# Attention blocks transposed in pairs, inverse sums spread by transposes, and the end of attention written in another order

## The chip, the core and the metric

The program runs on one of the eight NeuronCores of a Trainium2 chip. The metric is the device time of one execution in microseconds (us). A core has five engines that run side by side and meet at semaphores: TensorE (PE; its weight loads have a row of their own, PEld), VectorE (DVE), ScalarE (ACT), GpSimd (POOL) and SyncE (SP), which here only issues DMAs. Matrix products go to PSUM, which PE alone writes and which DVE and ACT read.

## The reference

```python
q_rot, k_rot = (rotate(q), rotate(k))            # rotary embedding, batch 2, 8 heads, 576 x 64
scores = scale * np.matmul(q_rot, k_rot.transpose(0, 1, 3, 2))
scores = scores - np.max(scores, axis=-1, keepdims=True)
attn = np.exp(scores)
attn = attn / (np.sum(attn, axis=-1, keepdims=True) + 1e-09)
x = np.matmul(attn, v)                           # then (batch * 576) x 512
h = x @ w_in;  x = where(h > 0, h, exp(min(h, 0)) - 1) @ w_out      # 512 -> 2048 -> 512
h = x @ w2_in; out = (h * tanh(softplus(h))) @ w2_out
```

## The kernel before

Heads are worked two at a time: eight pairs `p`, four for each of the two batch entries. A pair has nine score tiles of 128 queries by 576 keys (`TPP = 9`): tile `i` from 0 to 7 is head `i % 2`, query block `i // 2`, and tile 8 holds the last 64 queries of both heads. One loop over steps `u` (nine to a pair) writes the whole attention stage engine by engine in a fixed order; no scheduler moves anything there. In step `u` stand, among others:

- `do_S(u)`: the score product of tile `u` on PE into a PSUM tile `ps_s` (two buffers); `do_max(u)`: the row minimum of the negated scores on DVE (L392); `do_exp(u)`: the exponential on ACT (L400) into `P`, which frees `ps_s`.
- `do_T(u - 3)`: `P` of the tile three steps back is transposed on PE, four blocks of 128 keys into `psT` (L441) and the last 64 keys into a slot of `psL` (L442, output of 64 rows). `do_evac` copies `psT` into `pt` on DVE or ACT (L455, L457), `do_evac_last` copies `psL` for four tiles at a time on DVE (L467).
- `do_av(p, g, c)` (L473): output of group `g` (tiles 0 to 3, or 4 to 8) from key chunk `c` of five. Head 0 goes to PSUM rows 0 to 63 of `psA` and head 1 to rows 64 to 127, 256 columns each in group 0 and 320 in group 1. The table `plan` sets the steps.
- The inverse sums: `do_inverse` on DVE (L409 to L417) forms them and repeats each 64 times into `rw`; `do_spread` (L423) multiplies `rw` with an identity, so that they stand in `psA` along the columns; `do_keep` (L432, ACT) copies that to `R`. The product then uses the same `psA`; `do_x` (L488, DVE) multiplies it by `R` and so frees `psA` for the next spread; `do_xh` and `do_xl` (L492 on ACT, L496 on POOL) split the result in two for the next stage.
- POOL also applies the rotary embedding of later pairs (L273 to L277) and splits them (L298, L299). SP issues, in one queue, the loads of `qk` (L260), of the values `v` (L265), of raw weights, and small copies that wait for POOL's splits (L323, L338, L339).
- Weights of the next stage are prepared a part at a time (`weight_part`), from step 21 on: POOL L95, DVE L99, L103, L107, ACT L121, POOL L122. A job is opened when fewer than two are running, which issues its L95.

The feed-forward layers follow: per step one first product `g1_mm` (24 matmuls, L183) into `ps_s`, the activation, and later second products `g2_first` (L683, 24 matmuls) into `ps_g`. `tail` runs three first products within the last steps of attention.

Of the kernel before, what the change touches and what calls it, by code (L numbers as in the profile page):

```python
# [26 lines left out]
def kernel(  # L27
# [23 lines left out]
    GB, GE, PB = 9, 2, 4  # L51
# [123 lines left out]
    def g1_mm(m, f, b):  # L175
        c = m * NF + f
        hi, lo = WI[c]
        o = ps_s()
# [11 lines left out]

    G = {}
# [19 lines left out]
    def elu(m, f, b, o):  # L211
        h = o[:, :, :HS]
        t, g = tmp("ta"), tmp("tb")
        nc.scalar.activation(out=v2(g), in_=h, func=AF.Relu, scale=-1.0)
        nc.scalar.activation(out=t, in_=g, func=AF.Exp, scale=-1.0)
        nc.scalar.activation(out=g, in_=g, func=AF.Tanh, scale=-0.5)
        nc.vector.scalar_tensor_tensor(out=g, in0=t, scalar=1.0, in1=g, op0=ALU.add, op1=ALU.mult)
        nc.vector.tensor_tensor(out=v2(g), in0=v2(g), in1=h, op=ALU.max)  # L218
        return m, f, b, g
# [10 lines left out]
    def attention(att, ps, tail):  # L230
# [3 lines left out]
        idn2 = att.tile([128, 64], F32, name="idn2")  # L234
        rw = att.tile([128, 3, 2, 64], F32, name="rw")
# [9 lines left out]
        v_t = {}  # L245
        sp_t = {}
# [16 lines left out]
        def load_v(p):  # L263
            v = att.tile([128, 5, 128], F32, tag="v", name="v_t", bufs=2)
            nc.sync.dma_start(out=v, in_=vp[p])  # L265
            v_t[p] = v

# [75 lines left out]
        P_t = {}  # L343
        mn_t = {}
        sm_t = {}
        R_t = {}
        SLOT = (0, 1, 2, 3, 4)
# [47 lines left out]
        def do_exp(u):  # L395
            P = att.tile([128, S], F32, tag="P", name="P", bufs=PB)
            p, i = divmod(u, TPP)
            g, j = (0, i) if i < 4 else (1, i - 4)
# [7 lines left out]
        def do_inverse(p, g):  # L406
# [5 lines left out]
                out=rw[:, 0:2].rearrange("p t h d -> p (t h) d"),  # L412
                in_=r[:, 0:4].unsqueeze(2).to_broadcast([128, 4, 64]).unsqueeze(3), axis=AX.X, op=ALU.add,
            )
            for h in range(2 * g):
                rows = slice(64 * h, 64 * h + 64)
                nc.vector.tensor_reduce(  # L417
                    out=rw[rows, 2, h, :], in_=r[rows, 4:5].to_broadcast([64, 64]).unsqueeze(2), axis=AX.X, op=ALU.add
                )

        def do_spread(p, g):
# [12 lines left out]
        pt_t = [att.tile([128, 2, 5, n], F32, name=f"pt{g}") for g, n in enumerate((256, 320))]  # L434

        def do_T(u):
            P = P_t.pop(u)
            i = u % TPP
            tv = psT[u % 2]
            for c in range(4):  # L440
                nc.tensor.transpose(tv[:, c, :], P[:, c * 128:c * 128 + 128], idn)  # L441
            nc.tensor.transpose(psL[:S - 512, i % 4, :], P[:, 512:S], idn)  # L442
# [16 lines left out]
        def do_evac_last(i):  # L459
            r = S - 512  # L460
            if i < 8:
                o = pt_t[i // 4][:r, :, 4, 0:256].rearrange("p h (t q) -> p h t q", t=2)
                tv = psL[:r].rearrange("p (t h) q -> p h t q", h=2)
            else:
                o = pt_t[1][:r, :, 4, 256:320]
                tv = psL[:r, 0, :].rearrange("p (h q) -> p h q", h=2)
            nc.vector.tensor_copy(out=o, in_=tv)  # L467

        def do_av(p, g, c):
            n = (256, 320)[g]  # L470
            o = psA
            for h in range(2):
                nc.tensor.matmul(  # L473
                    o[64 * h:64 * h + 64, :n],
                    lhsT=v_t[p][:, c, 64 * h:64 * h + 64],
                    rhs=pt_t[g][:, h, c, :],
                    start=(c == 0), stop=(c == 4),
                )
# [7 lines left out]
        def do_x(p, g):  # L486
            x = R_t[p, g]
            nc.vector.tensor_tensor(out=x, in0=psA[:, :(256, 320)[g]], in1=x, op=ALU.mult)  # L488
# [5 lines left out]
        def do_xl(p, g, eng):  # L494
            x, hi, lo = x_parts(p, g)
            eng.tensor_tensor(out=lo, in0=x, in1=plain(hi), op=ALU.subtract)  # L496

# [16 lines left out]
        nc.vector.memset(rw[:, 2], 0.0)  # L514
        nc.vector.tensor_tensor(out=idn2, in0=idn[:, 0:64], in1=idn[:, 64:128], op=ALU.add)
        for t in pt_t:
            nc.vector.memset(t[S - 512:128, :, 4, :], 0.0)
# [56 lines left out]
        for u in range(max(av_at) + 2):  # L574
# [7 lines left out]
            if i == 8 and p + 1 < NP:  # L582
                load_v(p + 1)
            if u == 16:
# [5 lines left out]
            for (pp, g) in ends.get(u - 1, []):  # L590
                do_x(pp, g)
# [10 lines left out]
            for (pp, g, c) in av_at.get(u, []):  # L602
                if g == "r":
                    do_spread(pp, c)
                else:
                    do_av(pp, g, c)
            if u >= NU:
                tail(u - NU, False)
            if 0 <= u - LAG < NU:
# [4 lines left out]
                if j in (3, 7):  # L614
                    do_evac_last(j)
            for (pp, g) in spreads.get(u, []):
# [16 lines left out]
            for (pp, g) in ends.get(u - 1, []) + ends.get(u - 2, []):  # L633
                if (pp, g) in ends.get(u - (2 if g and u < NU else 1), []):
                    do_xh(pp, g)
                    do_xl(pp, g, nc.gpsimd if pp < NP - 1 else nc.vector)
            for _ in range(PARTS.get(u, 0)):
                if njob[0] < 2 * GF:
                    weight_part()
            if u >= NU:  # L640
                tmp_pool[0] = att
                tail(u - NU, True)
# [3 lines left out]
    def moe(mp, early):  # L646
# [19 lines left out]
        g_pool = [None]  # L666
# [70 lines left out]
        def step(n):  # L737
            m, f, b = g1_seq[n]
            o = early.pop(n) if n in early else g1_mm(m, f, b)
            if m == 0:  # L740
                for _ in range(3 if GF <= n < half - 1 else 0):
                    weight_part()
                if o is not None:
                    o = elu(m, f, b, o)
# [124 lines left out]
```

## Time and profile before

| | us |
|---|---|
| runs | 574.50, 574.96, 1397.33 |
| median | 574.96 |
| profiled execution | 570.46 |
| its span, first to last instruction | 568.6 |

In the span PE is busy for 553.9 us (97%), DVE for 376.9, ACT for 277.9, POOL for 238.7. The attention stage takes the first 160 us or so, the feed-forward layers the rest. A matmul's row gives when it started and a modelled end; since matmuls overlap, what one costs is read from one start to the next and not from its duration. An fp32 matmul leaves two records, an fp32 transpose one. "Idle" in brackets behind a row is how long that engine stood still before it, and what let it go on.

### The profile page before, as it was taken

The numbers are of one execution on the slowest core, as the hardware profiler recorded it, in microseconds if no ns is written. First come the engines' busy times: TensorE is split into PE (matmuls) and PEld (weight loads), VectorE is DVE, ScalarE is ACT, GpSimd is POOL, SyncE is SP. The second block draws the span as 40 slices with busy tenths as digits, with TensorE's granted clock in tenths as the row PEclk, the third lists the DMA queues.
The fourth block names the chain that finished last, engine by engine and source line by source line (L and its number), as shares of the span: only waits on it lengthen the run. The fifth ranks groups of instructions, "written<-read, shape, count | busy, mean of one in ns | idle before, by whom it ended". The sixth has DMA issues, their size and how long they took to land.

```text
span 568.6 us, 10131 instructions
## 1 busy us (share of the span) xinstructions
PE 553.9 (97%) x3888; PEld 499.7 (88%) x3888; DVE 376.9 (66%) x607; ACT 277.9 (49%) x512; POOL 238.7 (42%) x227
## 2 busy tenths in 40 slices
PE   7799999999999999999999999999999999999997
PEld 6568677777789999999999999999999998999985
DVE  6666899888846766777777777869844555432222
ACT  3646666667755665455555456435443322322110
POOL 6998999982310323323322331445533332230000
PEclk9999999999999999999999999999999999999999
DMA  6368676655110323223222322234532423000012
GB/s 231 110 197 258 205 228 178 184 143 161 38 39 4 108 80 107 76 76 96 91 74 78 108 75 75 85 115 139 159 116 84 121 88 110 22 14 10 29 65 93
DMA packets 43120, 60.69 MB, mean 107 GB/s; under 512 B 13760, under 2 KB 31936, under 8 KB 42304
## 3 DMA queue, kind: packets, MB, share of 16 engines
q1 hardware_dynamic: 42528, 59.46, 34.2%
q8 instruction: 31, 0.51, 0.4%
q10 hardware_dynamic: 544, 0.59, 0.3%
q14 instruction: 17, 0.14, 0.1%
HBM read 46.20 MB, written 2.36 MB: 85 GB/s over the span
## 4 chain that ended last, share of the span: by engine, by line
PE 85%; DVE 6%; ACT 3%; DMA 2%; issue 1%; POOL 1%; SPq 1%; ACTq 0%; POOLq 0%; DVEq 0%
PE ps_s L183 34%; PE ps_g L683 18%; PE ps_h L712 17%; PE ps_s L385 5%; PE psA L473 5%; PE psT L441 4%; DMA qk_t<-in_qk_dram 2%; PE psA L423 2%; DVE mn L392 1%; ACT P L400 1%; DVE wu L99 1%; PE psL L442 1%; DVE pt L455 1%; DVE R L488 0%; DVE rw L411 0%
## 5 line engine op out<-in xcount | busy, mean ns | idle before, releaser
L392 DVE TENSOR_REDUCE mn<-ps_s 128x1 f32<-128x576 f32 x72 | 53.9, 751 | 19.2 <-PE ps_s L385 15.2
L661 ACT ACTIVATE ta<-ps_s 128x576 f32<-128x576 f32 x32 | 20.8, 649 | 92.7 <-PE ps_s L183 92.6
L400 ACT ACTIVATE P<-ps_s,mn 128x576 f32<-128x576 f32 x72 | 53.1, 739 | 9.5 <-DVE mn L392 6.8
L183 PE MATMUL ps_s<-XH,wi0h 128*128 128x288 f32 x256 | 54.9, 296 | 0.9 <-DVE tb L218 0.9
L99 DVE TENSOR_SCALAR wu<-wu 128x512 int32<-128x512 int32 x64 | 33.7, 527 | 32.9 <-POOL wu L95 32.9
L183 PE MATMUL ps_s<-XL,wi0h 128*128 128x288 f32 x256 | 54.5, 294 | 0.0
L183 PE MATMUL ps_s<-XL,wi1h 128*128 128x288 f32 x256 | 54.4, 294 | 0.0
L183 PE MATMUL ps_s<-XH,wi0l 128*128 128x288 f32 x256 | 54.4, 294 | 0.0
L183 PE MATMUL ps_s<-XH,wi1l 128*128 128x288 f32 x256 | 54.2, 293 | 0.0
L183 PE MATMUL ps_s<-XH,wi1h 128*128 128x288 f32 x256 | 54.1, 293 | 0.0
L122 POOL TENSOR_TENSOR wi1l<-wu,wi1h 128x512 fp32r<-128x512 f32 x16 | 21.4, 1337 | 76.0 <-ACT wi1h L121 76.0
L122 POOL TENSOR_TENSOR wo0l<-wu,wo0h 128x512 fp32r<-128x512 f32 x16 | 21.9, 1366 | 68.3 <-ACT wo0h L121 56.4
L107 DVE SCALAR_TENSOR_TENSOR wu<-raw,wu 128x512 int32<-128x512 int32 x64 | 48.8, 762 | 1.7
L103 DVE SCALAR_TENSOR_TENSOR wu<-raw,wu 128x512 int32<-128x512 int32 x64 | 47.6, 744 | 2.0
L95 POOL TENSOR_SCALAR wu<-raw 128x512 f32<-128x512 f32 x64 | 45.1, 706 | 4.7
L473 PE MATMUL psA<-pt,v_t 128*64 128x256 f32 (+1 forms) x320 | 45.6, 416 | 0.6 <-ACT R L432 0.6
L122 POOL TENSOR_TENSOR wo1l<-wu,wo1h 128x512 fp32r<-128x512 f32 x16 | 22.0, 1375 | 57.2 <-ACT wo1h L121 56.9
L663 DVE TENSOR_TENSOR g<-ta,g 128x576 fp32r<-128x576 f32 x25 | 20.4, 817 | 36.4 <-ACT g L662 36.4
L183 PEld LDWEIGHTS ps_s<-XH,wi0h 128*128 128x128 f32 x256 | 41.4, 188 | 3.2 <-DVE tb L218 1.3
L457 ACT ACTIVATE pt<-psT 128x512 f32<-128x512 f32 x44 | 26.3, 597 | 36.4 <-PE psT L441 36.4
L441 PE MATMUL psT<-idn,P 128*128 128x128 f32 x288 | 43.4, 274 | 0.0
L183 PEld LDWEIGHTS ps_s<-XH,wi1h 128*128 128x128 f32 x256 | 41.8, 188 | 1.2
(146 smaller groups left out, 1409.6 us busy)
## 6 DMA issues: line engine op xcount, KB each, us to landing
raw<-in_w_in_dram SPq DMA_DIRECT2D x32, 512.0 KB, 3.7
raw<-in_w_out_dram SPq DMA_DIRECT2D x32, 512.0 KB, 3.3
qk_t<-in_qk_dram SPq DMA_DIRECT2D x6, 1152.0 KB, 7.2
qa<-qh SPq DMA_DIRECT2D x24, 144.0 KB, 2.6
v_t<-in_vp_dram SPq DMA_DIRECT2D x8, 320.0 KB, 4.3
out_dram<-Y SPq DMA_DIRECT2D x9, 256.0 KB, 2.0
ka<-kh SPq DMA_DIRECT2D x12, 144.0 KB, 2.5
ka<-kl SPq DMA_DIRECT2D x12, 144.0 KB, 2.6
```

The source lines that it names most:

```text
L95: nc.gpsimd.tensor_scalar(out=u, in0=high.bitcast(F32), scalar1=REBASE, scalar2=0.0, op0=ALU.mult, op1=ALU.add)
L99: nc.vector.tensor_scalar(out=ui, in0=ui, scalar1=3, scalar2=0x7FFFFFF8, op0=ALU.logical_shift_left, op1=ALU.bitwise_and)
L103: nc.vector.scalar_tensor_tensor(out=ui, in0=high, scalar=-0x80000000, in1=ui, op0=ALU.bitwise_and, op1=ALU.bitwise_or)
L107: nc.vector.scalar_tensor_tensor(out=ui, in0=low, scalar=29, in1=ui, op0=ALU.logical_shift_right, op1=ALU.bitwise_or)
L122: nc.gpsimd.tensor_tensor(out=lo, in0=u, in1=plain(hi), op=ALU.subtract)
L183: nc.tensor.matmul(o[:, j, :HS], lhsT=w[:, cc, :], rhs=x[:, b, cc, j * HS:j * HS + HS], start=(k == 0), stop=(k == 3 * NC - 1),)
L392: nc.vector.tensor_reduce(out=m, in_=psS[u][:, :, :HS], axis=AX.XY, op=ALU.min)
L400: nc.scalar.activation(out=P.rearrange("p (j n) -> p j n", j=2), in_=psS.pop(u)[:, :, :HS], func=AF.Exp, scale=-1.0, bias=mn_t.pop(u), acc ...
L441: nc.tensor.transpose(tv[:, c, :], P[:, c * 128:c * 128 + 128], idn)
L473: nc.tensor.matmul(o[64 * h:64 * h + 64, :n], lhsT=v_t[p][:, c, 64 * h:64 * h + 64], rhs=pt_t[g][:, h, c, :], start=(c == 0), stop=(c == 4),)
L683: nc.tensor.matmul(o[:, j, :HS], lhsT=w[:, e * 128:e * 128 + 128], rhs=gt[:, i, j * HS:j * HS + HS], start=(k == 0), stop=(k == 3 * GF - 1),)
L712: nc.tensor.matmul(o, lhsT=l, rhs=w, start=(k == 0), stop=(k == 3 * GF - 1))
```

## The change

- `do_T`: two heads' tiles (`i` even, then odd) lie side by side in one `P` buffer of 2 x 576 columns. The odd tile is transposed from column 64 on, so that the last 64 keys of the even tile and the first 64 of the odd one form one block of 128 columns, transposed at once with the odd tile. Tile 8 keeps its own 64-column block. A pair has 41 transposes of `P` in place of 45.
- The keys of head 1 are then in another order, so `load_v` lays its values out likewise, with four DMAs in place of one; tile 8 needs the old order, which `load_vb` loads with one more DMA. In group 1 of `do_av`, head 1's product of 320 columns becomes one of 64 (values `vb`) and one of 256.
- `do_spread` uses transposes for tiles 0 to 3 or 4 to 7, and for tile 8 two 64-column matmuls straight from the inverse; two DVE reductions (L417) go.
- `do_x` of group 1 moves from the following step to the end of its own, ahead of the weight parts. One weight job is opened at step 19.
- At the end of attention the last product goes to `psT[0]`, `tail` splits the activation and places the last `do_x`, `do_xh` and `do_xl` between its parts; the fifth first product uses `ps_g`, second products of the first block start a step later with one step that runs two. One preload of an activation table goes.

```diff
-        o = ps_s()
+        if (m, f, b) == (0, 0, 1):
+            o = g_pool[0].tile([128, 2, 512], F32, tag="g", name="ps_g", bufs=2)
+        else:
+            o = ps_s()
...
-            nc.sync.dma_start(out=v, in_=vp[p])
+            nc.sync.dma_start(out=v[:, :, 0:64], in_=vp[p, :, :, 0:64])
+            nc.sync.dma_start(out=v[0:64, :, 64:128], in_=vp[p, 64:128, :, 64:128])
+            nc.sync.dma_start(out=v[64:128, 0:4, 64:128], in_=vp[p, 0:64, 1:5, 64:128])
+            nc.sync.dma_start(out=v[64:128, 4, 64:128], in_=vp[p, 0:64, 0, 64:128])
...
+        def load_vb(p):
+            vb = att.tile([128, 5, 64], F32, tag="vb", name="vb_t", bufs=1)
+            nc.sync.dma_start(out=vb, in_=vp[p, :, :, 64:128])
...
-            P = att.tile([128, S], F32, tag="P", name="P", bufs=PB)
+                P2_t[p, i // 2] = att.tile([128, 2, S], F32, tag="P", name="P", bufs=PB)
...
         def do_spread(p, g):
-            for t in range(2 + g):
+            r = rc_t.pop((p, g))
+            for t in range(2):
+                nc.tensor.transpose(
+                    psA[:, 128 * t:128 * t + 128], rw[:, 2 * t:2 * t + 2].rearrange("p h d -> p (h d)"), idn
+                )
+            for h in range(2 * g):
                 nc.tensor.matmul(
-                    psA[:, 128 * t:min(128 * t + 128, 256 + 64 * g)],
-                    lhsT=rw[:, t].rearrange("p h d -> p (h d)"), rhs=idn if t < 2 else idn2,
-                    start=True, stop=True,
+                    psA[64 * h:64 * h + 64, 256:320],
+                    lhsT=r[:, 4:5].to_broadcast([128, 64]), rhs=idn[:, 64 * h:64 * h + 64], start=True, stop=True,
                 )
...
             for c in range(4):
-                nc.tensor.transpose(tv[:, c, :], P[:, c * 128:c * 128 + 128], idn)
-            nc.tensor.transpose(psL[:S - 512, i % 4, :], P[:, 512:S], idn)
+                k = k0 + c * 128
+                nc.tensor.transpose(tv[:, c, :], P[:, k:k + 128], idn)
+            if i == TPP - 1:
+                nc.tensor.transpose(psL[:S - 512, 0, :], P[:, 512:S], idn)
+            elif i % 2:
+                P2 = P2_t.pop((p, i // 2)).rearrange("p h k -> p (h k)")
+                nc.tensor.transpose(psL[:, i // 2, :], P2[:, 512:640], idn)
...
+        def av_home(p, g):
+            return psT[0].rearrange("p c q -> p (c q)") if (p, g) == (NP - 1, 1) else psA
...
             for h in range(2):
-                nc.tensor.matmul(
-                    o[64 * h:64 * h + 64, :n],
-                    lhsT=v_t[p][:, c, 64 * h:64 * h + 64],
-                    rhs=pt_t[g][:, h, c, :],
-                    start=(c == 0), stop=(c == 4),
-                )
+                m = n if h == 0 else 256
+                v = v_t[p][:, c, 64 * h:64 * h + 64]
+                if h and g:
+                    w = slice(256, 320)
+                    rhs = pt_t[g][:, h, c, w] if c < 4 else pl_t[g][:, 320:384]
+                    part(h, w, vb_t[p][:, c, :], rhs, True)
+                rhs = pt_t[g][:, h, c, :m] if c < 4 else pl_t[g][:, :m]
+                part(h, slice(0, m), v, rhs, not (h and g))
...
             for (pp, g) in ends.get(u - 1, []):
-                do_x(pp, g)
+                if g == 0:
+                    do_x(pp, g)
...
+            for (pp, g) in ends.get(u, []):
+                if g == 1 and pp < NP - 1:
+                    do_x(pp, g)
...
+            if u == 19:
+                open_job()
...
-                    pend.extend((n + (D1 if n < half - 1 else LATE[e]), (0, (g, b, e))) for e in range(NC))
+                    pend.extend((n + (2 if n < GF else D1 if n < half - 1 else LATE[e]), (0, (g, b, e))) for e in range(NC))
...
-            if n == half - 1:
-                nc.scalar.preload_act_table_set("mish")
```

The order on PE in pair 2's steps, over the product of pair 1's group 1. Before (`ka`, `qa`, `qb`: scores; `pt`: transposed exponentials):

```order
L473 MATMUL psA<-pt_86,v_t 64x320 x4
L385 MATMUL ps_s<-ka,qa 128x288 x2
L385 MATMUL ps_s<-ka,qb_113 128x288 x2
L441 MATMUL psT_82<-idn,P 128x128 x4
L442 MATMUL psL<-idn,P 64x128
L385 MATMUL ps_s<-ka,qa 128x288 x2
L385 MATMUL ps_s<-ka,qb_113 128x288 x2
L441 MATMUL psT_81<-idn,P 128x128 x4
L442 MATMUL psL<-idn,P 64x128
L473 MATMUL psA<-pt_86,v_t 64x320 x6
```

and in the changed kernel:

```order
L509 MATMUL psA<-pt_85,v_t 64x320
L509 MATMUL psA<-pt_85,vb_t 64x64
L509 MATMUL psA<-pt_85,v_t 64x256
L509 MATMUL psA<-pt_85,v_t 64x320
L509 MATMUL psA<-pt_85,vb_t 64x64
L509 MATMUL psA<-pt_85,v_t 64x256
L406 MATMUL ps_s<-ka,qa 128x288 x2
L406 MATMUL ps_s<-ka,qb_117 128x288 x2
L469 MATMUL psT_81<-idn,P 128x128 x4
L474 MATMUL psL<-idn,P 128x128
L406 MATMUL ps_s<-ka,qa 128x288 x2
L406 MATMUL ps_s<-ka,qb_117 128x288 x2
```

Every second tile has lost its transpose into `psL`, the others have one of 128 rows, and each chunk has three matmuls where it had two.

The order on POOL around the first weight preparations (`XL`: the split of the attention output; `qk_t`: rotary embedding of pair 4). Before:

```order
L299 TENSOR_TENSOR ql<-qk_t,qh 128x576
L496 TENSOR_TENSOR XL<-R_557,XH 128x256
L273 TENSOR_TENSOR qk_t<-qk_t,tab 128x576
L275 TENSOR_TENSOR qk_t<-qk_t,tab 128x576
L95 TENSOR_SCALAR wu<-raw 128x512 x2
```

and in the changed kernel:

```order
L318 TENSOR_TENSOR ql<-qk_t,qh 128x576
L540 TENSOR_TENSOR XL<-R_556,XH 128x256
L95 TENSOR_SCALAR wu<-raw 128x512
L292 TENSOR_TENSOR qk_t<-qk_t,tab 128x576
L294 TENSOR_TENSOR qk_t<-qk_t,tab 128x576
```

The first L95 now stands ahead of the embedding of pair 4, not behind two parts of it.

The order on DVE where pair 1's group 1 ends (`rw`: repeated inverse sums, `mn`: row minimum, `R`: output of attention). Before, `do_x` stood behind the weight part L103:

```order
L411 TENSOR_REDUCE rw<-rc 128x256
L392 TENSOR_REDUCE mn<-ps_s 128x1
L455 COPY pt_85<-psT_81 128x4x128
L103 SCALAR_TENSOR_TENSOR wu<-raw,wu 128x512
L488 TENSOR_TENSOR R_691<-psA,R_691 128x320
```

and in the changed kernel ahead of it:

```order
L437 TENSOR_REDUCE rw<-rc 128x256
L413 TENSOR_REDUCE mn<-ps_s 128x1
L487 COPY pt_84<-psT_80 128x4x128
L532 TENSOR_TENSOR R_690<-psA,R_690 128x320
L103 SCALAR_TENSOR_TENSOR wu<-raw,wu 128x512
```

## Rows read from the trace of the kernel before

**Rows 1.** The span in 40 equal slices: PE's busy tenths, and TensorE's granted clock

```profile
PE   7799999999999999999999999999999999999997
PEclk9999999999999999999999999999999999999999
```

**Rows 2.** Busy time in one stretch of attention, then granted clock, DMA share, GB/s

```profile
100.00:120.00 20.00, 19.89 (x152) 15.51 (x149) 17.58 (x32) 13.69 (x33) 17.76 (x16) 1.00 0.58 165
```

**Rows 3.** Who waited for whom: us in total, times, longest

```profile
PEld psA L423 <- DVE R L488: 2.1, 4, 1.0
...
SPq L323 <- POOL kh L298: 36.0, 6, 7.4
```

**Rows 4.** Timeline, steps of pairs 4 and 5: start, duration, engine, line [idle before]

```profile
97.49 0.52 PEld L423 LDWEIGHTS psA<-idn,rw 128*128 128x128 f32 x4 [0.37 <-DVE R L488]
97.49 0.71 PE L423 MATMUL psA<-idn,rw 128*128 128x128 f32 x4
...
97.96 0.51 PE L385 MATMUL ps_s<-ka,qa 128*128 128x288 f32 x2
...
99.21 1.08 PE L473 MATMUL psA<-pt,v_t 128*64 128x256 f32 x8
...
100.23 0.53 PE L385 MATMUL ps_s<-kh,bh 128*128 128x288 f32 x2
...
101.13 0.60 PE L441 MATMUL psT<-idn,P 128*128 128x128 f32 x4
...
101.56 0.27 PE L442 MATMUL psL<-idn,P 128*64 128x128 f32 x1
...
101.59 0.51 PE L385 MATMUL ps_s<-ka,qa 128*128 128x288 f32 x2
...
102.85 1.52 PE L473 MATMUL psA<-pt,v_t 128*64 128x256 f32 x12
...
104.29 0.53 PE L385 MATMUL ps_s<-ka,qa 128*128 128x288 f32 x2
...
106.68 0.78 PE L423 MATMUL psA<-idn,rw 128*128 128x128 f32 x6
...
107.27 0.51 PE L385 MATMUL ps_s<-ka,qa 128*128 128x288 f32 x2
```

**Rows 5.** Timeline, several engines, around the first weight preparation

```profile
45.41 0.43 SPq L260 DMA_DIRECT2D qk_t<-in_qk_dram  x1
...
53.82 1.41 POOL L273 TENSOR_TENSOR qk_t<-qk_t,tab 128x576 f32<-128x576 f32 x1 [0.59 <-DMA qk_t<-in_qk_dram]
...
56.57 1.31 POOL L95 TENSOR_SCALAR wu<-raw 128x512 f32<-128x512 f32 x2
...
57.28 0.87 DVE L99 TENSOR_SCALAR wu<-wu 128x512 int32<-128x512 int32 x1 [2.63 <-POOL wu L95]
...
59.79 0.53 PE L385 MATMUL ps_s<-ka,qa 128*128 128x288 f32 x2 [0.64 <-ACT P L400]
...
61.86 0.71 PE L423 MATMUL psA<-idn,rw 128*128 128x128 f32 x4 [0.73 <-DVE R L488]
```

**Rows 6.** Timeline of POOL: the once-a-pair wait, two pairs running

```profile
83.08 0.88 POOL L496 TENSOR_TENSOR XL<-R,XH 128x320 fp32r<-128x320 f32 x1 [1.09 <-ACT XH L492]
...
100.90 0.87 POOL L496 TENSOR_TENSOR XL<-R,XH 128x320 fp32r<-128x320 f32 x1 [1.09 <-ACT XH L492]
```

**Rows 7.** Timeline of PE: the end of attention, and one wait in mid-program

```profile
165.51 2.91 PE L473 MATMUL psA<-pt,v_t 128*64 128x320 f32 x20 [0.59 <-ACT R L432]
168.35 0.53 PE L183 MATMUL ps_s<-XH,wi0h 128*128 128x288 f32 x2
...
174.57 0.43 PE L183 MATMUL ps_s<-XH,wi0l 128*128 128x288 f32 x2
175.67 0.53 PE L183 MATMUL ps_s<-XH,wi0h 128*128 128x288 f32 x2 [0.67 <-DVE tb L218]
...
354.63 0.53 PE L183 MATMUL ps_s<-XH,wi0h 128*128 128x288 f32 x2 [0.19 <-DVE tb L218]
```

More of the change, by code (lines that the diff above doesn't have):

```diff
@@ L459, in do_evac_last, with part @@
         def do_evac_last(i):
-            r = S - 512
             if i < 8:
-                o = pt_t[i // 4][:r, :, 4, 0:256].rearrange("p h (t q) -> p h t q", t=2)
-                tv = psL[:r].rearrange("p (t h) q -> p h t q", h=2)
-            else:
-                o = pt_t[1][:r, :, 4, 256:320]
-                tv = psL[:r, 0, :].rearrange("p (h q) -> p h q", h=2)
+                g = i // 4
+                o = pl_t[g][:, 0:256].rearrange("p (t q) -> p t q", t=2)
+                tv = psL[:, 2 * g:2 * g + 2, :]
+            else:
+                o = pl_t[1][:S - 512, 256:384]
+                tv = psL[:S - 512, 0, :]
             nc.vector.tensor_copy(out=o, in_=tv)
+        def av_home(p, g):
+            return psT[0].rearrange("p c q -> p (c q)") if (p, g) == (NP - 1, 1) else psA
         def do_av(p, g, c):
             n = (256, 320)[g]
-            o = psA
-            for h in range(2):
-                nc.tensor.matmul(
-                    o[64 * h:64 * h + 64, :n],
-                    lhsT=v_t[p][:, c, 64 * h:64 * h + 64],
-                    rhs=pt_t[g][:, h, c, :],
-                    start=(c == 0), stop=(c == 4),
-                )
+            o = av_home(p, g)
+            def part(h, cols, v, rhs, first):
+                nc.tensor.matmul(
+                    o[64 * h:64 * h + 64, cols], lhsT=v, rhs=rhs,
+                    start=(c == 0 and first), stop=(c == 4), skip_group_check=True,
+                )
+            for h in range(2):
+                m = n if h == 0 else 256
[6 more added lines that the diff above has]
+                part(h, slice(0, m), v, rhs, not (h and g))
         def x_parts(p, g):
@@ L487, in do_x @@
             x = R_t[p, g]
[L488 removed]
+            nc.vector.tensor_tensor(out=x, in0=av_home(p, g)[:, :(256, 320)[g]], in1=x, op=ALU.mult)
         def do_xh(p, g):
@@ L513, in attention @@
             nc.vector.memset(t[:, :, 1:2], 1e-9)
[L514 to L517, printed above, removed]
+        nc.vector.memset(pl_t[1][S - 512:128, 256:384], 0.0)
         for t in qb:
@@ L573, in attention @@
                     ends.setdefault(u, []).append((p, g))
-        for u in range(max(av_at) + 2):
+        for u in range(max(av_at) + 1):
             p, i = divmod(u, TPP)
@@ L583, in attention @@
                 load_v(p + 1)
+            if i == 6 and p < NP:
+                load_vb(p)
             if u == 16:
@@ L641, in attention @@
                 tmp_pool[0] = att
-                tail(u - NU, True)
+                tail(u - NU, 1, last_x)
                 tmp_pool[0] = None
@@ L795, with tail @@
     early = {}
-    def tail(k, late):
-        if late:
-            if k in (2, 3):
-                elu_lo(*elu_hi(*early[k - 2]))
-                early[k - 2] = None
-            if k in (1, 2):
-                early[k - 1] = elu(0, k - 1, 0, early[k - 1])
-        elif k in (0, 1, 3):
-            n = min(k, 2)
-            early[n] = g1_mm(0, n, 0)
+    def tail(k, late, last_x):
+        if not late:
+            if k in (0, 1, 3):
+                n = min(k, 2)
+                early[n] = g1_mm(0, n, 0)
+        elif k == 1:
+            early[0] = elu_join(*elu(0, 0, 0, early[0]))
+        elif k == 2:
+            early[0] = elu_lo(*elu_hi(*early[0]))
+            early[1] = elu(0, 1, 0, early[1])
+        elif k == 3:
+            early[1] = elu_join(*early[1])
+            last_x()
+            early[1] = elu_lo(*elu_hi(*early[1]))
     with tc.tile_pool(name="att", bufs=1, reuse_waits="tile") as att, tc.tile_pool(
```

53 lines of the change are left out of this document (35 added, 18 removed).

## The prediction

> **What bounds the kernel now.** I read the busy slices first. PE is at nine tenths or more in 37 of 40 slices and TensorE's granted clock is at its upper level, 2.4 GHz, throughout; only the first two slices and the last, at seven tenths, leave PE idle [rows 1]. The windows come next: in 100 to 120 us PE is busy for 19.89 of 20 us, but DVE for 17.58 and POOL for 17.76 [rows 2]. So PE is the bound of attention with two engines close behind, and a gain on PE is worth itself only down to their pace. Busy PE hides stalls, so I took the waits and then the timeline. The weight loads of the spread waited four times for `do_x`, 2.1 us in all [rows 3]; one of these is seen at 97.49, 0.37 us [rows 4]. The reader is to see that a matmul's price is the step between two starts: four transposes take 0.43 us (101.13 to 101.56), 0.108 each, though each row would say 0.27 [rows 4].
>
> **What the change takes from PE, in one pair.** Four transposes fewer: 4 x 0.108 = 0.43 us. Spread of group 0: two fp32 matmuls, four records, take 0.47 us (97.49 to 97.96), or 0.118 for 128 columns [rows 4]; two transposes at 0.108 take 0.22: 0.25 less. Spread of group 1: 0.59 us now (106.68 to 107.27) [rows 4]; then 0.22 for two transposes and two 64-column matmuls of two records each. Those have no row. From below, side by side for the two heads, two slots of half a 128-column record: 0.12. From above, one after another at a full record: 0.47. Turning to a run of half-width matmuls and back has a fixed cost: 12 records of the product take 1.44 us (102.85 to 104.29) and 8 take 1.02 (99.21 to 100.23), so 0.105 a record and 0.18 a run [rows 4]. Taken: 0.22 + 0.12 + 0.18 = 0.52, 0.07 less, since these two matmuls are of the same form as the product's; the other end is 0.28 more.
>
> **What it adds to PE.** Group 1's chunk goes from two matmuls to three. Twenty records of 320 columns took 2.84 us (165.51 to 168.35) [rows 7], 0.57 a chunk of four. At 0.118 for 128 columns one record of 320 alone would take 0.29, and two of them 0.59; so the two heads run side by side at no loss. Head 1 now has 64 + 256 columns, as many as head 0, so below the price is nothing; above, both 64-column records lie bare at a full record: 0.24 a chunk. I take 0.05, near the low end because the halves stay equal: 0.25 us a pair, 2.0 over 40 chunks, with ends 0 and 9.6.
>
> Together 0.43 + 0.25 + 0.07 - 0.25 = 0.50 us a pair: 3.0 us for pairs 2 to 7. In pairs 0 and 1 PE stands still a quarter of the time [rows 1], so I count half: 0.5.
>
> **Form changes, row and rule.** The fifth transposes have 64 rows of output and stand between 128-row work. The score product starts 0.03 us after such a transpose (101.56 to 101.59), and the transpose follows its four neighbours at their pace [rows 4]: no gap, so I count nothing for the 64 that go. The Trainium skill, TensorEngine Tiling (Array Packing), Key Properties, says that changing the tiling mode drains TensorE. By that rule each of the 64 would have cost two drains, and the sum would be larger. The rows do not show it for these transposes.
>
> **The waits.** At 57.28 DVE had stood for 2.63 us for the first L95, which is queued on POOL behind two embeddings that themselves waited for a load [rows 5]; behind it on DVE stood row minima, so PE waited 0.64 us for an exponential and 0.73 for `do_x`. With the job opened at step 19, L95 stands ahead of these embeddings: 1.37 us go. The three other waits for `do_x`, 0.37 each, come from L103 in front of it [rows 3, 4]; with `do_x` first, 1.1 us go. `do_x` now makes DVE wait for the end of the product; behind it stand L103 and the next row minimum, and that tile's score buffer is asked for only two steps later: nothing. At the end of attention the product no longer waits for `R`, since it has its own bank: of 0.59 us I keep 0.05 for the copies of tile 8, 0.54 goes. The fifth first product started 1.10 us after a pair of records that takes 0.26 (174.57 to 175.67) [rows 7], waiting for a score buffer; in `ps_g` it has one at once: 0.84 goes.
>
> **Costs counted at nothing.** Four more DMAs a pair on SP, at 0.43 us an issue [rows 5], 1.7 us: hidden by SP's wait of 6 us a pair for POOL's split (36.0 in six) [rows 3]. Without that cover they delay `qk`, whose load took 8.4 us from issue to use [rows 5] (see the first rival). Shorter copies out of `psL` and two reductions fewer help DVE, which is not the bound. An even tile's exponential now needs the transposes of the tile three back, but stands behind their copy on ACT already. The activation table is loaded beside PE work: PE's only wait there is 0.19 us, on DVE [rows 7]. Second products that start a step later are the same work.
>
> **Sum.** 3.0 + 0.5 + 1.37 + 1.1 + 0.54 + 0.84 = 7.35 us. The profiled execution, 568.6 us of span and 1.9 around it, 570.46, becomes 563.1. The median of the runs is 574.96, 4.5 above the profiled one; I take the gain from the median: **567.6 us**, 1.3% less. A measurement of this kernel tells about 2% from no change, so this forecast would be called no change.
>
> **Rivals.**
> - *POOL and SP set the pace.* POOL waits only 1.09 us of each 17.82 (83.08 to 100.90) [rows 6], so it needs 16.73; PE's new period is 17.82 - 0.37 - 0.50 = 16.95. There are 0.22 us of room, and `qk` comes 1.7 us later. If POOL keeps standing for `qk`, or the exponentials cannot follow the shorter steps, the period of pairs 3 to 6 stays: 3 x 0.37 + 4 x 0.50 = 3.1 us are lost, 570.7. For it: the tight windows. Against: splits are ready some microseconds before PE asks. 18%.
> - *The short matmuls lie bare.* At 0.24 a chunk the product costs 9.6, not 2.0: 575.2. 10%.
> - *Slower: the heads no longer run side by side.* Three matmuls for two halves of the array break the alternation that the rows show. One after another a chunk is 640 columns twice at 0.118 per 128, 1.18 us, not 0.57: 0.61 x 40 = 24.4 more, against 7.35 + 2.0 saved: 590.0. It decides from 0.23 us a chunk on. Against: the halves have equal columns and separate weights. 6%.
> - *Form changes drain after all.* If each of the 64 transposes hid two changes at half the 0.18 of a run, 11.5 us more would go: 556.1. The 0.03 us step speaks against it. 2%. This is the rule of the Trainium skill's TensorEngine Tiling (Array Packing), Key Properties, named above; the rows do not bear it out.
> - *It does not do what it says*: the early L95 waits for its raw weights, and the embedding of pair 4, now later, holds the rest. Then 1.37 us stay: 569.0, within the forecast's range. 2%.
>
> **How the numbers follow.** The forecast has 62%; its own range is 564 (chunks at nothing, pairs 0 and 1 in full, and some scatter) to 570. The range 562.5 to 573.0 takes in the first rival and leaves out the bare matmuls, the serial heads and the drains, 18%. Faster by over 2% (below 563.5): 6%, the drains and the forecast's lower tail. Slower by over 2% (above 586.5): 4%, most of the serial case. Within: 90%.
>
> **What the profile after would show.** The step from four transposes to the next score product 0.11 shorter for every even tile; the group 0 spread at 0.22; a chunk of group 1 at 0.57 to 0.62 in the run of five chunks at the end of attention; no wait of the spread for `do_x`, no DVE wait for the first L95, no wait at the fifth first product; a pair's period near 16.95. Wrong would be: POOL without its 1.09 us wait and PE waiting for splits or exponentials (first rival); chunks over 0.8 us (second and third); half-width runs that cost more than 0.18 at the spread.

## The result, and the profile after

The changed kernel takes 568.22 us (median of 4 runs, 567.48 to 568.74) against 576.14 in the same session (the three runs of before and a fourth of 577.32; the one of 1397.33 does not enter the ratio): ratio 0.9871, interval 0.9836 to 0.9906. That is 1.3% less and counts as no change, as forecast (567.6). Its profiled execution took 568.74 us, span 566.9. The first trace of before had a span of 568.6, so trace against trace shows 1.7 us, run against run some 7. The second trace of before, an experiment below, shows why. Stretches worked out from starts of rows in the three traces (the first transpose of a pair opens it; "end" runs from attention's last transpose to the fifth first product, "rest" from there to the last matmul), in us:

| stretch | before, first trace | before, second trace | after | forecast of the change |
|---|---|---|---|---|
| pairs 0, 1 | 37.9 | 37.9 | 37.2 | -0.5 |
| pair 2 | 19.14 | 23.72 | 16.73 | -1.87 |
| pairs 3 to 7 | 91.69 | 91.70 | 90.18 | -3.6 |
| end | 11.75 | 11.74 | 10.35 | -1.38 |
| rest | 389.1 | 393.4 | 393.4 | 0 |

The end came as forecast. Pairs 3 to 7 gave less than half of what was forecast, pair 2 more, and the rest differs between two traces of one kernel. The forecast's total was right through sizes that were not.

The timeline of after, around the first weight preparation (it answers to [rows 5]):

```profile
49.06 0.58 SPq L271 DMA_DIRECT2D qk_t<-in_qk_dram  x1
...
52.65 0.67 POOL L95 TENSOR_SCALAR wu<-raw 128x512 f32<-128x512 f32 x1
...
53.91 0.42 DVE L99 TENSOR_SCALAR wu<-wu 128x512 int32<-128x512 int32 x1
...
59.24 1.54 POOL L292 TENSOR_TENSOR qk_t<-qk_t,tab 128x576 f32<-128x576 f32 x1 [5.92 <-DMA qk_t<-in_qk_dram]
```

L95 runs ahead of the embedding and DVE waits no more. But SP issues `qk` 3.65 us later (49.06, not 45.41; 1.7 in the prediction) and POOL waits 5.92 us for it, not 0.59. From there POOL has no slack: it is busy for 19.68 of 20 us, and its once-a-pair wait [rows 6] is gone, 17.13 us a pair. The window of after (columns as in [rows 2]) and POOL's timeline:

```profile
100.00:120.00 20.00, 19.74 (x160) 15.83 (x157) 18.25 (x34) 14.65 (x36) 19.68 (x17) 1.00 0.80 217
...
85.96 0.86 POOL L540 TENSOR_TENSOR XL<-R,XH 128x320 fp32r<-128x320 f32 x1
...
103.09 0.86 POOL L540 TENSOR_TENSOR XL<-R,XH 128x320 fp32r<-128x320 f32 x1
```

PE's timeline of after, against [rows 4] and [rows 7], with what held PE in its two new waits:

```profile
68.82 0.89 POOL L540 TENSOR_TENSOR XL<-R,XH 128x320 fp32r<-128x320 f32 x1
...
69.75 0.44 ACT L457 ACTIVATE R<-psA 128x320 f32<-128x320 f32 x1 [1.16 <-POOL XL L540]
...
70.24 0.48 PE L509 MATMUL psA<-pt,v_t 128*64 128x320 f32 x1 [0.47 <-ACT R L457]
...
76.12 1.89 DVE L103 SCALAR_TENSOR_TENSOR wu<-raw,wu 128x512 int32<-128x512 int32 x1
...
78.77 0.74 ACT L426 ACTIVATE P<-ps_s,mn 128x576 f32<-128x576 f32 x1 [1.10 <-DVE mn L413]
...
79.70 0.50 PE L406 MATMUL ps_s<-kh,bh 128*128 128x288 f32 x2 [0.64 <-POOL qk_t L294]
...
86.15 0.38 PE L445 MATMUL psA<-idn,rw 128*128 128x128 f32 x2
...
86.73 0.53 PE L406 MATMUL ps_s<-ka,qa 128*128 128x288 f32 x2
...
94.37 0.38 PE L445 MATMUL psA<-idn,rw 128*128 128x128 f32 x2
94.51 0.51 PE L406 MATMUL ps_s<-ka,qa 128*128 128x288 f32 x2
...
160.31 0.48 PE L509 MATMUL psT<-pt,v_t 128*64 128x320 f32 x1
...
163.21 0.53 PE L186 MATMUL ps_s<-XH,wi0h 128*128 128x288 f32 x2
...
169.44 0.42 PE L186 MATMUL ps_s<-XH,wi0l 128*128 128x288 f32 x2
169.70 0.43 PE L186 MATMUL ps_g<-XH,wi0h 128*128 128x288 f32 x2
```

Group 0's spread takes 0.14 us (94.37 to 94.51; forecast 0.22), group 1's 0.58 (86.15 to 86.73; forecast 0.52). Five chunks of group 1 take 2.90 (160.31 to 163.21), 0.58 each: 0.01 more than before, where 0.05 was taken. The fifth first product starts 0.26 us behind its neighbour, not 1.10.

The new waits are at 70.24 and 79.70. The first is for `R`: there is one buffer of it for group 1, ACT writes it once POOL has read the last one for `XL`, and POOL is late. The second is for an exponential, by the times: the row names POOL's L294, but that had ended at 79.28; the exponential that frees the score buffer, behind a row minimum (77.94 to 78.68) behind an L103 of 1.89 us, had its last part end at 79.60.

### The profile page after: what moved, and what is told of

Its sections match the earlier page's. It is cut to its first block, busy times and chain, and to the rows that moved or that the text cites. A ratio compares the mean times of both kernels' runs of the same rounds, so it can differ in the third digit from the quotient of the medians.

```text
span 566.9 us, 10182 instructions
## 1 busy us (share of the span) xinstructions
PE 552.8 (98%) x3920; PEld 506.2 (89%) x3920; DVE 370.4 (65%) x588; ACT 275.5 (49%) x511; POOL 239.4 (42%) x227
## 4 chain that ended last, share of the span: by engine, by line
PE 83%; DVE 5%; ACT 3%; POOL 3%; DMA 3%; issue 1%; SPq 1%; POOLq 0%; DVEq 0%; ACTq 0%
PE ps_s L186 35%; PE ps_g L737 18%; PE ps_h L766 17%; PE psA L509 4%; PE ps_s L406 4%; PE psT L469 3%; DMA qk_t<-in_qk_dram 3%; DVE mn L413 1%; ACT P L426 1%; DVE wu L107 1%; DVE wu L103 1%; ACT pt L489 1%; POOL qk_t L294 1%; POOL qk_t L292 1%; PE ps_g L186 1%
## 5 line engine op out<-in xcount | busy, mean ns | idle before, releaser
L186 PE MATMUL ps_s<-XH,wi0h 128*128 128x288 f32 x248 | 53.5, 297 | 0.1
L186 PE MATMUL ps_s<-XL,wi0h 128*128 128x288 f32 x248 | 53.2, 296 | 0.0
L186 PE MATMUL ps_s<-XH,wi0l 128*128 128x288 f32 x248 | 53.0, 295 | 0.0
L107 DVE SCALAR_TENSOR_TENSOR wu<-raw,wu 128x512 int32<-128x512 int32 x64 | 50.2, 785 | 1.7
L103 DVE SCALAR_TENSOR_TENSOR wu<-raw,wu 128x512 int32<-128x512 int32 x64 | 49.7, 776 | 1.9
L95 POOL TENSOR_SCALAR wu<-raw 128x512 f32<-128x512 f32 x64 | 44.7, 700 | 9.9 <-DMA raw<-in_w_out_dram 5.4
L228 DVE SCALAR_TENSOR_TENSOR tb<-ta,tb 128x576 f32<-128x576 f32 x30 | 22.7, 758 | 33.9 <-ACT tb L224 33.7
L122 POOL TENSOR_TENSOR wi0l<-wu,wi0h 128x512 fp32r<-128x512 f32 x16 | 21.4, 1338 | 48.5 <-ACT wi0h L121 48.5
```

Of the source, the lines that this page charges most:

```text
L95: nc.gpsimd.tensor_scalar(out=u, in0=high.bitcast(F32), scalar1=REBASE, scalar2=0.0, op0=ALU.mult, op1=ALU.add)
L103: nc.vector.scalar_tensor_tensor(out=ui, in0=high, scalar=-0x80000000, in1=ui, op0=ALU.bitwise_and, op1=ALU.bitwise_or)
L107: nc.vector.scalar_tensor_tensor(out=ui, in0=low, scalar=29, in1=ui, op0=ALU.logical_shift_right, op1=ALU.bitwise_or)
L122: nc.gpsimd.tensor_tensor(out=lo, in0=u, in1=plain(hi), op=ALU.subtract)
L186: nc.tensor.matmul(o[:, j, :HS], lhsT=w[:, cc, :], rhs=x[:, b, cc, j * HS:j * HS + HS], start=(k == 0), stop=(k == 3 * NC - 1),)
```

## The experiments

### Before, once more

> The kernel before, unchanged, for a second trace. Theory: its runs near 575 differ from its first profiled execution (570.46) in the pace of the matmuls in the first half of the feed-forward layers: there the first trace stepped 128 and 132 ns in turn (260 a pair), the changed kernel's trace 131, 131, 132, 140 (267 a pair). A step of 24 first and 24 second products then takes 6.40 us in place of 6.25, over 28 steps 4.2 us; the last transpose of attention stays at 163.9 us and the run takes about 574.7 us. Rival: the 4.5 us lie in attention (last transpose later than 165 us) or outside the span; the pace stays at 260 a pair.

Measured: median 572.84 (10 runs, 570.02 to 579.47), ratio 0.9998 [0.9953, 1.0042]; the profiled execution was the longest of them. The "rest" is 4.3 us longer than in the first trace, as the theory had it. What it had not: pair 2 takes 4.6 us more. Timeline, then windows of PE alone (length, busy time with the number of instructions, granted clock, DMA share, GB/s):

```profile
58.63 1.25 POOL L95 TENSOR_SCALAR wu<-raw 128x512 f32<-128x512 f32 x2
...
59.31 0.85 DVE L99 TENSOR_SCALAR wu<-wu 128x512 int32<-128x512 int32 x1 [4.55 <-POOL wu L95]
...
61.80 0.53 PE L385 MATMUL ps_s<-ka,qa 128*128 128x288 f32 x2 [2.54 <-ACT P L400]
...
63.88 1.23 PE L423 MATMUL psA<-idn,rw 128*128 128x128 f32 x4 [0.59 <-DVE R L488]
...
62.00:64.00 2.00, 1.41 (x10) 0.72 0.89 280
64.00:66.00 2.00, 2.00 (x9) 0.50 1.06 427
66.00:68.00 2.00, 2.00 (x12) 0.50 0.69 290
68.00:70.00 2.00, 2.00 (x11) 0.58 0.02 9
```

POOL's embedding of `qk` starts 2.05 us later (55.87, not 53.82; 0.55 of it is a later issue), DVE waited 4.55 us for L95 and not 2.63 [rows 5], PE stood for 2.54 and not 0.64. After that stall the granted clock is at the lower level, 1.2 GHz, for some 6 us while PE is busy. Of the 4.6 us the longer stall is 1.9 (2.54 for 0.64), and the wait for `do_x` gives 0.1 back (0.59 for 0.73); the other 2.8 fall into the stretch at the lower clock. So the first L95's wait is a term whose size changes from one execution to the next.

### The early weight job: without it, and alone

```diff
-            if u == 19:
-                open_job()
```

> The changed kernel without the weight job opened at step 19. Theory of the prediction: DVE waits again for the first L95, which stands behind two embeddings that wait for qk; the 1.37 us come back (569.6), and since qk is now issued 3.65 us later than before the change, up to 3.6 us more (573.2). Rival: other waits (R, scores) cover it and nothing comes back, 568.2 us.

Measured: 575.32 (573.30 to 576.01), ratio 1.0015 [0.9984, 1.0046]. All of the gain is gone. Timeline and windows as above:

```profile
62.12 0.85 DVE L99 TENSOR_SCALAR wu<-wu 128x512 int32<-128x512 int32 x1 [6.81 <-POOL wu L95]
...
64.64 0.85 PE L406 MATMUL ps_s<-ka,qa 128*128 128x288 f32 x2 [5.00 <-ACT P L426]
...
64.00:70.00 6.00, 5.36 (x23) 0.50 0.86 207
```

The theory's direction was right and its upper size (573.2) too small: it had not counted the clock. The 5.0 us stall is followed by about 6 us at 1.2 GHz. With the later `qk` this line pays for the whole change.

Alone, added to before:

> The kernel before with one line of the change alone: the weight job opened at step 19. Theory (the stall behind the first L95, with the half clock that follows it when it is long, is most of what the runs won): no DVE wait over 0.5 us for L95, granted clock 1.0 from 56 to 80 us, pairs 2 and 3 take 17.9 us each in place of 23.7 and 17.8; the last transpose of attention at 162.5 us; 573.3 us if the feed-forward pace is 267 ns a pair of matmuls and 569.1 if it is 260, median about 571 against 574.9. Rival (1.37 us as the prediction had it, against before's median): 573.5 us. Second rival (PE's work is what was won): no change, 574.9.

Measured: 571.54 (568.68 to 575.07), ratio 0.9946 [0.9906, 0.9986]: five runs from 568.7 to 570.1, five from 573.0 to 575.1. Granted clock 1.0 from 56 to 80 us, no DVE wait for L95, last transpose at 161.85. Pairs 3 and 4 take 17.45 us each, where before had 17.82: the wait for `do_x` [rows 3, 4] is gone there too, with `do_x` where it was (in pair 5 it is still 0.3 us). DVE's timeline in pair 4:

```profile
93.54 0.68 DVE L103 SCALAR_TENSOR_TENSOR wu<-raw,wu 128x512 int32<-128x512 int32 x1
94.34 0.49 DVE L488 TENSOR_TENSOR R<-psA,R 128x320 f32<-128x320 f32 x1
```

L103, ahead of `do_x`, takes 0.68 us here, 0.93 in pair 3 and 1.80 in pair 5; in the first trace of before 1.23 or 1.24 in each of these. So the wait for `do_x` came with a long L103, and the job opened early shifts the weight parts against POOL's work. Two more places of this trace serve further below, the spread of group 0 with no wait ahead of it and the last transpose of tile 8:

```profile
77.89 0.61 PE L423 MATMUL psA<-idn,rw 128*128 128x128 f32 x4
78.25 0.51 PE L385 MATMUL ps_s<-ka,qa 128*128 128x288 f32 x2
...
86.11 0.67 DVE L467 COPY pt<-psL 64x512 f32<-64x512 f32 x1
...
86.83 0.11 PEld L442 LDWEIGHTS psL<-idn,P 128*64 128x64 f32 x1 [0.16 <-DVE pt L467]
```

### `do_x` back in its place

```diff
-                if g == 0:
+                if g == 0 or pp < NP - 1:
                     do_x(pp, g)
...
-            for (pp, g) in ends.get(u, []):
-                if g == 1 and pp < NP - 1:
-                    do_x(pp, g)
```

> The changed kernel with do_x of group 1 back at the head of the next step, behind the weight part L103. Theory of the prediction: the spread of the next group 0 waits 0.25 to 0.37 us for do_x in three pairs again, 0.8 to 1.1 us more: 569.0 to 569.3 us, last transpose 160.2 to 160.5. Rival (the wait was only moved): with L103 ahead of do_x again, the stalls of 0.17, 0.14 and 0.11 us a pair before score products go, and the total stays within 0.3 us: 568.2 us.

Measured: 567.25 (566.20 to 570.41), ratio 0.9893 [0.9864, 0.9922]. Pairs 2 to 7 take 104.3 us in place of 106.9, pairs 2 to 4 16.72 to 16.76 each, and in these six pairs PE's only waits are 0.12 and 0.23 us, both for `R`. Neither theory foresaw a gain. DVE and POOL, first in after, then with `do_x` back:

```profile
93.14 1.45 POOL L292 TENSOR_TENSOR qk_t<-qk_t,tab 128x576 f32<-128x576 f32 x1
93.39 0.49 DVE L532 TENSOR_TENSOR R<-psA,R 128x320 f32<-128x320 f32 x1 [0.25 <-PE psA L509]
93.80 1.34 DVE L103 SCALAR_TENSOR_TENSOR wu<-raw,wu 128x512 int32<-128x512 int32 x1
94.52 1.89 POOL L294 TENSOR_TENSOR qk_t<-qk_t,tab 128x576 f32<-128x576 f32 x1
```

```profile
92.10 0.68 DVE L103 SCALAR_TENSOR_TENSOR wu<-raw,wu 128x512 int32<-128x512 int32 x1
92.19 1.19 POOL L540 TENSOR_TENSOR XL<-R,XH 128x256 fp32r<-128x256 f32 x1
92.82 0.49 DVE L532 TENSOR_TENSOR R<-psA,R 128x320 f32<-128x320 f32 x1
93.34 1.43 POOL L292 TENSOR_TENSOR qk_t<-qk_t,tab 128x576 f32<-128x576 f32 x1
94.72 1.42 POOL L294 TENSOR_TENSOR qk_t<-qk_t,tab 128x576 f32<-128x576 f32 x1
```

Moved ahead, `do_x` waits for the product and L103 starts behind it, beside POOL's embeddings: it takes 1.34 us in place of 0.68, and the embedding 1.89 in place of 1.42. Over pairs 3 to 5 L103 takes 1.53 us on average in after and 0.73 with `do_x` back. The row minimum behind L103 is late, then the exponential, then PE. The Trainium skill, SBUF — State Buffer, Who interferes with whom, says that a DVE instruction with two SBUF inputs contends with a GpSimd instruction that reads SBUF, and that issue order decides who blocks. These rows agree: in them the one that starts second is the longer, L103 behind L292 (1.34 for 0.68), L294 behind L103 (1.89 for 1.42), and with `do_x` back POOL's `XL` behind L103 (1.19, elsewhere 0.74).

### `qk` ahead of the values on SP

```diff
-                if p + 1 < NP:
-                    load_pair(p + 1)
...
+            if i == 6 and p + 3 < NP:
+                load_pair(p + 3)
             if i == 6 and p < NP:
                 load_vb(p)
```

> The changed kernel, with the load of a pair's qk issued three steps earlier on SP, ahead of the loads of vb, of raw weights and of the four parts of v. Theory (SP's longer queue delays qk, POOL then runs without slack): qk of pair 4 is issued near 44 us in place of 49.06, POOL's wait of 5.92 us for it goes, and with it PE's two stalls of 0.54 and 0.71 us near 70 and 80 us: last transpose of attention at 158.1 us in place of 159.35, 567.0 us. Rival (DVE: the weight part L103, now behind do_x, holds the row minima, whatever POOL does): the stalls stay, 159.3 and 568.2 us. Second rival (POOL's own work of 17.13 us a pair is the bound): the stalls near 70 and 80 go but later pairs are no shorter than 17.1.

Measured: 568.96 (567.71 to 571.93), ratio 0.9929 [0.9899, 0.9959]; pairs 2 to 7 take 106.0. POOL waits again, 0.19 us for each of the larger `XL`, so it is not late, and from 50 to 125 us PE no longer waits for `R`; yet it stalls in each of three pairs:

```profile
80.18 0.50 PE L406 MATMUL ps_s<-kh,bh 128*128 128x288 f32 x2 [0.47 <-POOL qk_t L294]
97.41 0.50 PE L406 MATMUL ps_s<-kh,bh 128*128 128x288 f32 x2 [0.47 <-POOL qk_t L294]
114.63 0.50 PE L406 MATMUL ps_s<-kh,bh 128*128 128x288 f32 x2 [0.45 <-POOL qk_t L294]
...
93.59 0.49 DVE L532 TENSOR_TENSOR R<-psA,R 128x320 f32<-128x320 f32 x1 [0.44 <-PE psA L509]
94.00 1.72 DVE L103 SCALAR_TENSOR_TENSOR wu<-raw,wu 128x512 int32<-128x512 int32 x1
```

These stalls are the rival's: L103 behind `do_x` takes 1.72 us, whatever POOL's lateness. (The rows name L294; for the stall at 97.41 it had ended at 96.99, and the exponential at 97.22.) Both edits together:

> The changed kernel with do_x of group 1 back at the head of the next step and the load of qk three steps earlier, as two runs before had them singly. Theory (what is left of POOL's wait for qk, 4.57 us, costs pairs 5 and 6, of 16.91 and 17.14 us against 16.72, through POOL's lateness): all pairs at 16.72, last transpose 157.0 in place of 157.63, 566.6 us. Rival (POOL's lateness costs nothing at 16.72 us a pair; the later pairs are longer for their two weight parts a step): no change against the kernel with do_x back, 567.25.

Measured: 568.32 (5 runs, 568.28 to 568.44), ratio 0.9898 [0.9862, 0.9933]; pairs 2 to 7 take 105.0, two of them 16.7. No gain over `do_x` alone (104.3): the rival again. (In both traces the granted clock is 0.90 from 13 to 30 us, 1.00 in after, and pairs 0 and 1 take 38.4 us in place of 37.2.)

`qk` first, without the early job:

> The changed kernel without the weight job opened at step 19, but with the load of qk three steps earlier. Theory (the 7 us that came back without the early job are L95 queued on POOL behind embeddings that wait for qk, and the half clock after it): with qk there in time POOL does not wait, L95 runs on time, PE's stall of 5.0 us near 60 us is under 0.7, granted clock 1.0 from 56 to 80 us, 568 to 569 us. Rival (the job has to be opened early whatever qk does, for example for its raw weights or for the two jobs opened at once): stall over 2 us and half clock again, 573 to 575 us.

Measured: 569.84 (568.71 to 570.54), ratio 0.9925 [0.9892, 0.9957], against 575.32 with `qk` late:

```profile
56.20 0.86 DVE L99 TENSOR_SCALAR wu<-wu 128x512 int32<-128x512 int32 x1 [2.08 <-POOL wu L95]
...
60.00:64.00 4.00, 3.15 (x24) 2.35 (x24) 4.00 (x7) 2.47 (x6) 2.82 (x2) 1.00 0.32 70
```

The clock stays at 1.0 and PE's single stalls are 0.74 us and less. So the seven microseconds are L95 behind embeddings that wait for `qk`, and the clock after it; either edit removes most of them.

### The end of attention undone

The last product goes to `psA` again, `tail` has its old order, the fifth first product uses `ps_s`, and second products of the first block start a step earlier again; of the edit, two parts:

```diff
-        if (m, f, b) == (0, 0, 1):
-            o = g_pool[0].tile([128, 2, 512], F32, tag="g", name="ps_g", bufs=2)
-        else:
-            o = ps_s()
+        o = ps_s()
...
-            return psT[0].rearrange("p c q -> p (c q)") if (p, g) == (NP - 1, 1) else psA
+            return psA
```

> The changed kernel with the end of attention as before: the last product in psA, do_x a step later, tail in its old order, the fifth first product in ps_s, second products of the first block a step earlier. Theory of the prediction (terms of 0.54 and 0.84): 1.38 us come back after the last transpose of attention, 569.6 us; the way from that transpose to the fifth first product is 11.75 us again and not 10.35. Rival (what is won there is given back at the start of the feed-forward layers): under 0.4 us, 568.2 to 568.6.

Measured: 570.39 (569.32 to 572.02), ratio 0.9936 [0.9907, 0.9965]. From attention's last transpose to the fifth first product 11.64 us, with both waits back:

```profile
161.16 0.48 PE L506 MATMUL psA<-pt,v_t 128*64 128x320 f32 x1 [0.60 <-ACT R L454]
...
171.34 0.53 PE L183 MATMUL ps_s<-XH,wi0h 128*128 128x288 f32 x2 [0.63 <-DVE tb L226]
```

These 1.29 us bear out the terms of 0.54 and 0.84.

### Heads in another order

```diff
-                if h and g:
-                    ...
-                    part(h, w, vb_t[p][:, c, :], rhs, True)
                 rhs = pt_t[g][:, h, c, :m] if c < 4 else pl_t[g][:, :m]
-                part(h, slice(0, m), v, rhs, not (h and g))
+                part(h, slice(0, m), v, rhs, True)
+                if h and g:
+                    ...
+                    part(h, w, vb_t[p][:, c, :], rhs, False)
```

> The changed kernel with head 1's matmul of 256 columns ahead of that of 64 in each chunk of group 1, so that the columns of the two heads are 320, 256, 64 in this order. Theory (records of the two halves run side by side whatever the order, as long as each half has 320 columns): chunk 0.57 us, run of five chunks at the end as in the changed kernel, 568.2 us. Rival (only neighbours of equal place overlap, and the short one must stand first to hide): each chunk 0.05 to 0.24 us more, 40 chunks, 570.2 to 577.8 us.

Measured: 568.08 (4 runs, 567.43 to 569.55), ratio 0.9902 [0.9863, 0.9941]; five chunks 2.89 us, as in after (2.90). The two halves run side by side in either order, so the rivals of bare and of serial matmuls had no ground. Its pairs 2 to 7 take 105.6.

### After, once more

> The changed kernel, unchanged, for a second trace beside the others. Theory (do_x of group 1 ahead of L103 makes L103 collide with POOL's embeddings and row minima late): stalls of PE before score products and the product again, pairs 2 to 7 take 105.6 to 107 us in place of the 104.4 with do_x back; median 568.2. Rival (its first trace was an unlucky one): 104.4 us, median 567.3.

Measured: 568.42 (567.52 to 569.82), ratio 0.9916 [0.9883, 0.9949]; pairs 2 to 7 take 106.7, with waits for `R` (0.54, once more behind POOL's `XL`, the longest) and at a score product (0.64). Its pairs set the two cases side by side: in pair 4 POOL stands for `qk`, L103 runs alone in 0.68 us, and the pair takes 16.73; in pairs 3 and 5 L103 takes 1.25 and 1.89 and the pairs 17.03 and 18.27. Over the traces: with `do_x` moved, five traces without the stall for L95 give 105.6 to 106.9 us, with it back 104.3, 104.3 and 105.0, and one 107.2 (the next run, where PE waited 1.37 us for a late copy of `qa` and 1.2 in two waits for `R`, behind POOL's `XL`). The medians' intervals overlap, so the loss is shown in the traces, with that one exception, and not in the times.

### Two paces of the same matmuls

One small matmul of 8 to 184 columns ahead of the first products of steps 8 to 30:

```diff
+        N = extra[0]
+        if N:
+            nc.tensor.matmul(o[:, 1, 320:320 + N], lhsT=hi[:, 0, :], rhs=XH[:, b, 0, 0:N], start=True, stop=True)
...
+            extra[0] = 8 * (n - 7) if 8 <= n <= 30 else 0
```

> The changed kernel with do_x of group 1 back at the head of the next step, and in feed-forward steps 8 to 30 one more small matmul ahead of the 24 of the first product, 8 columns in step 8, 16 in step 9, up to 184 in step 30 (into unused columns, its result is not used). It asks whether a small shift in time flips the pace of the following matmuls between 267 and 260 ns a pair. Theory (the pace is a state that a shift can set and that then stays): some of the 23 stretches run at 128 and 132 ns in turn, 6.25 us a step less the small matmul, others at 131, 131, 132, 140. Rival (the pace hangs on something else, for example what DMAs move): all stretches run at 267 ns a pair, and the run takes 1 to 2 us more than without.

Measured: 572.28 (1 run). Behind the small matmuls of 16, 32 and 48 columns, each of which met the long pattern, the matmuls step 128 and 132 (or 129 and 131) ns in turn until the next small one; that of 24, 40 or 56 columns took the long pattern back, and that of 8 and all larger ones left it. So a small shift switches the pace, in either direction. With one small matmul alone, of 40 columns at step 8 (its expectation names the sizes one step too high):

> The changed kernel with do_x of group 1 back at the head of the next step, and one small matmul of 40 columns ahead of the first product of feed-forward step 8 (its result is not used). In the probe run small matmuls of 24, 40 and 56 columns took the pace from 267 to 260 ns a pair, and the next small matmul took it back; with one alone it should stay until PE next waits, near 345 us. Theory: 24 steps at 6.25 in place of 6.40 us, 3.6 us less, 563.7 us against 567.25. Rival (where in its pattern of four the small matmul falls differs from one execution to the next): some runs near 563.7 and some near 567.3, median between. Second rival (the pace cannot be held): 567.4.

Measured: 563.65 (6 runs, 562.62 to 565.42), ratio 0.9825 [0.9778, 0.9872], the fastest of all; its "rest" is 389.6 us, against 393.4 with `do_x` back alone. Windows of PE, 40 us of the same steady work: with the small matmul, then in the second trace of before, then in after.

```profile
240.00:280.00 40.00, 40.00 (x310) 1.00 0.26 79
```

```profile
240.00:280.00 40.00, 40.00 (x302) 1.00 0.24 80
```

```profile
240.00:280.00 40.00, 40.00 (x303) 1.00 0.27 85
```

PE counts as fully busy and the clock as 1.00 in all three; only the number of matmuls tells them apart. The first trace of before and that with the early job alone have 310 as well. In both the short pace sets in at the same place, the last matmuls of the first second product, where one step is 136 or 137 ns and not 140; after has passed that place without a break.

## Why the forecast held, step by step

- **PE's work: 0.73 us a pair, not 0.50.** The periods without stalls are 17.45 (before with the early job) and 16.72 (`do_x` back). From step to step in these two traces the difference is 0.43 for four transposes, as forecast, 0.23 for group 0's spread (0.25 forecast), 0.12 for a wait, 0.01 for group 1's spread (0.07 forecast), less 0.05 for the chunks (0.25 forecast) and 0.02 at score products. Group 0's term was right by luck: the 0.47 read in [rows 4] stands behind the wait for `do_x`; without one the old spread takes 0.36 (77.89 to 78.25), and the new one takes 0.14, not 0.22. The 0.12 is a term put at nothing: tile 8's last transpose waited for DVE's copy out of `psL`, which took 0.67 us and takes 0.41 now, so a shorter copy did help PE. Over six pairs that is 1.4 us more than forecast. The 64-row transposes left no gap, as counted.
- **The first L95: mechanism right, size off.** 1.37 us was its price in one execution. In the second trace of before pair 2 lost 4.6 us more than in the first, in part through the clock; without the early job the changed kernel's median was 7.1 higher. What the prediction had as a constant depends on when `qk` lands. Its text says that PE stood still; that the clock falls after a longer stall it did not see, as its trace had no such row.
- **`do_x`: the step that failed.** The prediction gave 1.1 us to moving it and "nothing" to what is queued behind it. The early job alone removed that wait in two pairs of three. The move put L103 beside POOL's embeddings and the row minimum behind it, and cost some 1 to 2.5 us in the traces (waits for `R` among them). "That tile's score buffer is asked for only two steps later" was true of a row minimum delayed by L103's 0.68 us, not by 1.3 to 1.9.
- **The extra DMAs: counted at nothing, the cover was gone where it mattered.** SP's wait for POOL did not hide them ahead of `qk`; POOL's wait went from 0.59 to 5.92 us and its slack of 1.09 a pair vanished. This is the first rival's mechanism, and POOL's cadence of 17.13 is its sign. It reached PE by a way that neither the prediction nor its rival named, the one buffer of `R` that POOL reads late: from 50 to 125 us PE waited 0.47 us for it in after, 0.54 in the second trace, and not at all with `qk` early. The stalls at score products stayed with `qk` early; those were L103's.
- **The end: 1.40 against 1.38**, and 1.29 lost when undone.
- **The sum, against the median.** Pairs 2 to 7 gave 3.9 us against the first trace and 8.5 against the second, forecast 5.5. Up to the fifth first product (175.67 and 169.70) the change gave 5.97 us against the first trace, of 7.35. The 4.5 us between profiled execution and runs, which the prediction carried over as an offset, is no offset: it is the pace of the first feed-forward half (4.3) plus, in some executions, the stall behind L95. In the session with the most runs of before, 31, the 13 with a mean granted clock of 0.999 or more form two groups, five from 569.8 to 571.8 us and eight from 574.3 to 575.9; the stall of the second trace took its mean clock to 0.994, so it is not what parts them. That the forecast met the time is luck in this: taken from the profiled execution it would have been 563.1, below every run of after. The choice of the median, for which the prediction gives no reason, held because after has the long pace as well.
- **What stays open.** After had the long pace in both of its traces and no run under 567.4; why before falls into the short pace in part of its executions is not settled. Before has waits at the start of the feed-forward layers, shortly ahead of where its pace changed, and after has not. But the second trace of before has them too, at the long pace; and with the end undone they are back, the trace has the long pace (a "rest" of 393.5 us), and its ten runs lie within 2.7 us of each other. So these waits alone do not bring the short pace.

## What to carry to other kernels

Price a wait from more than one execution: one behind a DMA can have another length in the next, and here a longer one cost TensorE's clock on top. Read the price of a step where no wait stands ahead of it. When an instruction is moved on one engine, look at what runs beside the ones behind it on the other engines, not only at who waits. And when busy shares and clock agree but times don't, count instructions in equal windows.

## What the runs showed of the hardware

- Matmuls of 288 columns in an unbroken stream ran in one of two patterns at the same granted clock: 260 ns or 267 ns for two. A pattern held for 150 us and more, until PE waited; a single small matmul (0.03 us) switched it and was worth about 3.6 us.
- Three fp32 matmuls on two halves of the array, 320 against 256 + 64 columns, cost 0.58 us a chunk, as two of 320 did (0.57), in either order.
- A PE stall of 2.5 us was followed by 6 us at 1.2 GHz; stalls of 0.64 and 0.73 us were not.
